# Two feed-forward weight loads moved from behind the fourth key unit to behind the query weights

## The chip, the core and the metric

The kernel runs on one core of one Trainium2 chip, alone. The metric is the device time of one execution in microseconds (us); lower is better. Everything is float32.

## What is computed

One token (x, 512 numbers) goes through two branches, and a sigmoid gate mixes them. Cut from the reference to what matters:

```python
g = sigmoid((x * gate_w).sum())
q = (x @ wq)                                  # 32 query heads of 128; wq is 512 x 4096
scores = q . k_cache / sqrt(128)              # 8 key heads (4 queries share one), 32768 keys each
o = softmax(scores) @ v_cache                 # 8 value heads, 32768 x 128 each
a = o.reshape(4096) @ wo                      # wo is 4096 x 512
h = silu(x @ w1) * (x @ w3)                   # w1, w3 are 512 x 1792
b = h @ w2                                    # w2 is 1792 x 512
out = g * a + (1 - g) * b
```

The caches are by far the largest operands: 8 heads x 32768 x 128 x 4 bytes = 134 MB of keys and as much of values. All weights together are 28 MB. Each byte is read once.

## The kernel before

**Units.** Keys and values come from HBM in units of 8 MiB (128 partitions x 16384 floats), each as one DMA of the SP queue, and into one of two buffers: `big_a` and `big_b`, each of exactly one unit. There are 16 key units, written k0 to k15 here, and 16 value units, v0 to v15. Four key units make up two heads (index `w`, four of them); `t` runs over the key units. wq is as large as a unit and is loaded into `big_a`; w1 and w3 (3.5 MiB each) share `big_b`.

**Order of the loads before.** wq, k0, k1, k2, k3, w1, w3, k4, v0, k5, v1, and so on in turn up to k15 and v11; then v12 to v15, w2 and wo. The function `where(t)` (line 324) names the buffer of a key unit: k0 and k2 go to `big_b`, all others to `big_a`. Values go to `big_b`, the last four alternate. SP issues the loads in this order and waits before each one until the buffer's earlier content has been read.

**Work on one key unit** (`set_aside`, `scores`, lines 336 to 370). A unit has two halves (z = 0, 1) of four chunks. VectorE (DVE) transposes each chunk in 32 x 32 blocks into one of two small buffers (`kt`, one of them inside the tensor `aside`), and TensorE (PE) multiplies it with a window of query columns (`winc`) and sums into a PSUM bank. ScalarE (ACT) copies three of the second half's four chunks into `aside` as soon as the unit has landed, so that the load's buffer is free once DVE has done five of the eight transposes, and PE the five products. SP's next load into that buffer waits for this fifth product. For k3 alone the kernel before also has ACT copy the remaining chunk to an unused corner of `big_b` behind w3 (`extra`, line 340), since k3 and k4 both go to `big_a`.

**After four key units** PE transposes the finished scores (`turn`), and DVE takes the maximum and subtracts it (`softmax`, lines 397 to 421); ACT takes the exponential. The sum over the probabilities (`total`) follows after the next unit. Each engine works through its own list in the order in which the program adds the steps: DVE's part of a softmax stands ahead of its transposes of the next key unit.

**Lag.** `LAG` is 4: values are multiplied four units behind the keys. So PE's work has two loops: one over k0 to k3 without values (with a filler product, line 614, after every second chunk), one over k4 to k15, in which v0 to v11 are multiplied (`values_all`, line 445). A value load waits until PE has multiplied the content of `big_b`.

**The feed-forward branch.** `hidden_products` (line 475) multiplies x with w1 and w3, on PE; `hidden` (line 490) applies silu and the product, on ACT and DVE, and leaves the result for the end. Before, the loads stand behind k3, the products between PE's two loops, and `hidden` behind unit t = 4.

**Recording.** Steps are recorded by `Program.add`, which derives the waits from the names of what a step reads and writes, and are emitted per engine in the order of recording. Line 199 is the helper of nearly all loads of SP, line 432 issues the value units v0 to v11.

Of the kernel before, what the change touches and what calls it, by code (L numbers as in the profile page):

```python
# [118 lines left out]
def kernel(  # L119
# [13 lines left out]
    nc = tc.nc  # L133
    _, HKV, S, DH = k_cache.shape
    D = x.shape[-1]
    F = w1.shape[1]
    HQ = wq.shape[1] // DH
    REP = HQ // HKV
    NC = D // P
# [6 lines left out]
    NB = 64  # L146
    R = NB * DH
    NP = HKV // 2
    NH = 4 * NP
    LAG = 4  # L150
# [7 lines left out]
    pe, dve, act, pool = (  # L158
        lambda fn, _e=e, **kw: pr.add(_e, fn, **kw) for e in ("PE", "DVE", "ACT", "POOL")
    )  # L160
    V, A, T = nc.vector, nc.scalar, nc.tensor

    def sbuf(name, *shape):
        return nc.alloc_sbuf_tensor(name, [P, *shape], F32)[:]

    big = [sbuf("big_a", 2 * R), sbuf("big_b", 2 * R)]
# [28 lines left out]
    def load(dst, src, writes, over=()):  # L195
        lanes[0] += 1
        lane = f"load{lanes[0] % 9}"
        return pr.add(
            "SP", lambda: nc.sync.dma_start(dst, src), writes=writes, over=[*over, lane], inc=lane, by=16, also=lane,  # L199
        )  # L200

    def region(b, z):
        return big[b][:, z * R:(z + 1) * R]
# [7 lines left out]
    ident, ones, fold = sbuf("ident", P), sbuf("ones", P), sbuf("fold", 32)  # L211
# [1 line left out]
    spot, mask, xp = sbuf("spot", 8, 4, 4), sbuf("mask", 32), sbuf("xp", NC, 32)  # L213
    here, share, mine, weight = sbuf("here", 8, 4), sbuf("share", 8, 4), sbuf("mine", 32), sbuf("weight", 2)
    gate, sums, recip, on = sbuf("gate", 2), sbuf("sums", 32), sbuf("recip", 32), sbuf("on", 32)
    mt, mtt, mark, mark2 = sbuf("mt", 32), sbuf("mtt", 128), sbuf("mark", 1), sbuf("mark2", 1)
    high, top = sbuf("high", 1), sbuf("top", 32)
    G = nc.gpsimd
    pool(lambda: G.memset(acc, 0.0), writes=["acc"])  # L219
# [44 lines left out]
    def clear(**kw):  # L264
        pe(zeros,
           reads=["acc"], writes=["s"], **kw)
# [15 lines left out]
    for c in range(NC):  # L282
        def part(c=c):
# [18 lines left out]
         reads=["gate0"], writes=["gate1"])  # L302
# [4 lines left out]
    for b in range(2):  # L307
        qt = kt[b][:, 0:512]
        dve(lambda b=b, qt=qt: V.transpose(qt, rows[b]), reads=[f"row{b}"], writes=[f"kt{b}"])
        for j in range(4):  # L310
            w, u = divmod(4 * b + j, 2)
            src = qt[32 * j:32 * j + 32, :].rearrange("p (q c x) -> p x c q", q=4, c=4)[:, 0]
            for e in range(2):
                r, o = 2 * u + e, 16 + 8 * e + 4 * u
# [7 lines left out]
    vd = v_cache.rearrange("a h (e p n) d -> (a h) e p (n d)", e=2, p=P)  # L322

    def where(t):
        return 1 if t in (0, 2) else 0

    def load_keys(t):
        b = where(t)
        load(big[b], kd[t // 4, t % 4], ["AB"[b] + str(z) for z in range(2)])
# [1 line left out]


    spare = aside.rearrange("p (n r) -> p n r", n=NB)
    extra = big[1][:, 2 * NC * F:2 * R].rearrange("p (n r) -> p n r", n=NB)

    def set_aside(t):
        src, key = region(where(t), 1).rearrange("p (n r) -> p n r", n=NB), "AB"[where(t)] + "1"
        act(lambda: A.copy(spare, src[:, :, 32:128]), reads=[key], writes=["wo"])  # L338
        if t == LAG - 1:
            act(lambda: A.copy(extra, src[:, :, 0:32]), reads=[key], writes=["extra"], over=["B1"])  # L340

    def window(t, z):
        return act(
            lambda: A.copy(winc, win[:, t // 4, :, 16 - 16 * z:48 - 16 * z]),  # L344
            reads=[("win", t // 4, r) for r in range(4)], writes=["winc"], credit="windows",
        )

    def scores_part(c):
        for g in range(4):
            ins = T.matmul(  # L350
                ps_s[32 * g:32 * g + 32, :], winc[:, c, :], kt[c % 2][:, 512 * g:512 * g + 512],
                start=False, stop=False, skip_group_check=True,
            )
        return ins

    def scores(t, z, win_op):
        kin = region(where(t), z).rearrange("p (n c j) -> p c n j", c=4, j=32)
        ks = []
        for c in range(4):
            src, key = kin[:, c], "AB"[where(t)] + str(z)  # L360
            if (z, c) >= (1, 1):
                src, key = spare[:, :, 32 * (c - 1):32 * (c - 1) + 32], "wo"
            elif z == 1 and t == LAG - 1:
                src, key = extra, "extra"
            dst = kt[c % 2].rearrange("p (n i) -> p n i", i=32)
            k = dve(lambda d=dst, s=src: V.transpose(d, s), reads=[key], writes=[f"kt{c % 2}"],  # L366
                    over=["kt0"] * (t >= LAG and (z, c) == (1, 1)), credit="keys")
            pe(lambda c=c: scores_part(c), reads=[f"kt{c % 2}", "winc"], writes=["s"], loop=True,
               credits=((win_op, 1), (k, 1)) if c == 0 else ((k, 1),))
            ks.append(k)  # L370

        if t == LAG - 1 and z == 0:
            done = dve(lambda: V.tensor_copy(mark2, ones[:, 0:1]), reads=["ones"], writes=["mark2"])
            for k in ks:
                k.via = done

    def scores_out(t):
        o = act(
            lambda: A.copy(sb[:, :, :, t % 4], ps_s.rearrange("p (n i) -> p n i", i=32)),  # L379
            reads=["s"], writes=[("sb", t % 4)], credit="scores",  # L380
        )
        return o
# [9 lines left out]
    def turn(loop, credits=()):  # L392
        for f in range(4):
            pe(lambda f=f: turn_part(f), reads=[("sb", m) for m in range(4)] + ["ident"], writes=[f"f{f}"], loop=loop,
               credits=credits if f == 0 else ())
# [33 lines left out]

    def load_values(s):  # L430
        return pr.add(
            "SP", lambda: nc.sync.dma_start(big[1], vd[s // 2, s % 2]), writes=["B0", "B1"], over=["extra"],
            credit="values", by=16,
        )

# [35 lines left out]
    def load_hidden():  # L471
        for z, t in enumerate((w1, w3)):
            load(big[1][:, z * NC * F:(z + 1) * NC * F], t.rearrange("(p c) f -> p (c f)", c=NC), [f"B{z}"])

    def hidden_products():
        for z in range(2):
            def ff(z=z):
                t = big[1][:, z * NC * F:(z + 1) * NC * F]
                for c in range(NC):
                    for j in range(4):  # L480
                        o = c * F + FJ * j
                        ins = T.matmul(
                            pm[z][32 * j:32 * j + 32, 0:FJ], xp[:, c, :], t[:, o:o + FJ],
                            start=(c == 0), stop=(c == NC - 1),
                        )
                return ins
            pe(ff, reads=[f"B{z}", "xp"], writes=[f"m{z}"])


    def hidden():  # L490
        act(lambda: A.activation(silu[:, 0:FJ], pm[0][:, 0:FJ], AF.Sigmoid), reads=["m0"], writes=["tmp0"])
        dve(lambda: V.tensor_mul(silu[:, 0:FJ], silu[:, 0:FJ], pm[0][:, 0:FJ]), reads=["m0", "tmp0"], writes=["tmp0"])
        dve(lambda: V.scalar_tensor_tensor(
            prod[:, 0:FJ].rearrange("p (k a) -> p k a", k=FR), silu[:, 0:FJ].rearrange("p (a k) -> p k a", k=FR),
            gate[:, 1:2], pm[1][:, 0:FJ].rearrange("p (a k) -> p k a", k=FR), op0=ALU.mult, op1=ALU.mult,
        ), reads=["tmp0", "gate1", "m1"], writes=["tmp1"])
        dve(lambda: V.transpose(htp.rearrange("p k a -> p (k a)"), prod[:, 0:FJ]), reads=["tmp1"], writes=["htp"])
# [4 lines left out]
    def store(e, src, key, inc):  # L502
        i, q = (0, nc.scalar) if e == "ACT" else (1, nc.sync)
        pr.add(e, lambda: q.dma_start(outs[2 * i:2 * i + 2, :], src[31 + 64 * i:33 + 64 * i, :]),
               reads=[key], writes=[("out", i)], inc=inc, by=16)

    load_keys(0)
    vals = {}
    first = window(0, 0)
    for t in range(NH):  # L510
        v = t - LAG
        set_aside(t)
        scores(t, 0, first)
        scores(t, 1, window(t, 1))
        out_op = ((scores_out(t), 1),)
        if v < 0:
            clear(loop=True, credits=out_op)
        if t == LAG - 1:
            load_hidden()
        if t + 1 < NH:  # L520
            load_keys(t + 1)
            first = window(t + 1, 0)
        if v >= 1:
            own(v - 1)
        if t % 4 == 3:
            turn(v >= 0, out_op if v >= 0 else ())
        if v >= 0:
            values_loop(vals.pop(v), weights(v), () if t % 4 == 3 else out_op)
            clear(loop=True)
        if t == LAG - 1:  # L530
            hidden_products()
        if v + 1 >= 0 and t + 1 < NH:
            vals[v + 1] = load_values(v + 1)

        if t == NH - 1:
            pool(lambda: G.memset(otp, 0.0), writes=["otp"], over=["kt1"])
        if t % 4 == 3:
            softmax(t // 4)
        if t % 4 == 0 and t > 0:
            total(t // 4 - 1)  # L540
        if t == LAG:
            hidden()
    total(NP - 1)


# [89 lines left out]
    def down(ks):  # L635
# [9 lines left out]
        reads=[("each", 0), ("each", 1), "otp"], writes=["lay"])  # L645
# [38 lines left out]
    done = pr.semaphore("PE")  # L684
# [65 lines left out]
```

## Time and profile before

| | |
|---|---|
| Median of 3 runs | 694.33 us (693.72 to 694.63) |
| Profiled execution: its own time | 694.08 us |
| Span in its trace | 692.4 us |
| Bytes read from HBM | 296.23 MB, 428 GB/s over the span |
| PE / DVE / ACT busy | 402.8 / 368.4 / 134.6 us (58 / 53 / 19 % of the span) |
| SP's load queue | busy for 99.1 % of the span of 16 DMA engines |

In the page's part on queues the last number of a row is the time that the packets of a queue took, as a share of all 16 DMA engines over the span. Times inside a trace are counted from the span's start. A row of a timeline gives start, duration, engine, line, operation, out<-in with shapes, the count of merged instructions, and in brackets how long the engine had been idle and what released it. A load has two rows of interest: its issue on SP, and the first instruction that it released, whose start is called its landing here.

### The profile page before, as it was taken

Reading aid. Unit: us, or ns where it says so; the run is one execution under the profiler, and the core shown is the slowest. Engines: PE = TensorE matmul, PEld = TensorE weight load, DVE = VectorE, ACT = ScalarE, POOL = GpSimd, SP = SyncE. Lnnn points to the kernel's source line nnn. Section 1 sums busy time; section 2 is a strip of 40 time slices with the busy share of each in tenths; the row PEclk is TensorE's granted clock in tenths of the full one; section 3 lists DMA queues with packets and bytes.
Section 4 is the critical chain, followed back from the end, with each engine's and each line's share of the span. In section 5 each row is a group of like instructions: output and inputs, shape, how many; then the busy total and the mean of one; then the engine's idle time right before and its main releaser. Section 6 shows DMA issues by size and latency. Waiting matters only on the chain. (4 is left out here: it accounts for less than half of the span.)

```text
span 692.4 us, 5704 instructions
## 1 busy us (share of the span) xinstructions
PE 402.8 (58%) x2430; PEld 94.6 (14%) x2430; DVE 368.4 (53%) x229; ACT 134.6 (19%) x113; POOL 8.1 (1%) x34
## 2 busy tenths in 40 slices
PE   1537777566474656557484645666573646744575
PEld 0101111201010110201010101201010102211121
DVE  0049999394735637493726537593826546700026
ACT  0143223232303130220303131210303131100000
POOL 4000000000000000000000000000000000000000
PEclk9969999958667676977786777778586777776689
DMA  9999999999999999999999999999999999999996
GB/s 386 455 428 424 424 424 436 448 443 424 428 428 428 435 454 432 424 432 428 432 454 435 424 428 428 432 435 451 432 424 428 428 435 454 435 421 424 433 421 284
DMA packets 6068, 296.34 MB, mean 428 GB/s; under 512 B 678, under 2 KB 682, under 8 KB 1068
## 3 DMA queue, kind: packets, MB, share of 16 engines
q1 hardware_dynamic: 6052, 296.23, 99.1%
q8 instruction: 5, 0.08, 0.0%
q14 instruction: 3, 0.02, 0.0%
q10 hardware_dynamic: 8, 0.01, 0.0%
HBM read 296.23 MB, written 0.00 MB: 428 GB/s over the span
## 5 line engine op out<-in xcount | busy, mean ns | idle before, releaser
L366 DVE STREAM_TRANSPOSE aside<-big_a 128x2048 f32<-128x2048 f32 x41 | 94.3, 2300 | 166.9 <-DMA big_a<-in_A_k_cache_dram 166.9
L350 PE MATMUL ps<-aside,winc 128*32 128x512 f32 x512 | 96.0, 830 | 142.4 <-PEq L688 141.5
L350 PE MATMUL ps<-kt,winc 128*32 128x512 f32 x512 | 96.2, 832 | 61.2 <-PEq L688 61.2
L451 PE MATMUL ps<-big_b,pv 128*32 128x512 f32 x768 | 96.1, 657 | 17.5 <-PEq L688 17.5
L338 ACT COPY aside<-big_a 128x6144 f32<-128x6144 f32 x14 | 74.4, 5313 | 151.8 <-DMA big_a<-in_A_k_cache_dram 151.8
L366 DVE STREAM_TRANSPOSE kt<-aside 128x2048 f32<-128x2048 f32 x32 | 73.4, 2293 | 17.2 <-PE ps L350 17.2
L366 DVE STREAM_TRANSPOSE kt<-big_a 128x2048 f32<-128x2048 f32 x28 | 63.5, 2269 | 0.0
L379 ACT COPY sb<-ps 128x512 f32<-128x512 f32 x16 | 17.1, 1069 | 156.8 <-PE ps L350 156.8
L350 PEld LDWEIGHTS ps<-aside,winc 128*32 128x32 f32 x512 | 13.4, 125 | 215.7 <-issue 215.7
L451 PEld LDWEIGHTS ps<-big_b,pv 128*32 128x32 f32 x768 | 27.7, 120 | 88.1 <-issue 88.1
L366 DVE STREAM_TRANSPOSE aside<-aside 128x2048 f32<-128x2048 f32 x16 | 36.3, 2269 | 0.0
L583 DVE TENSOR_TENSOR sb<-ps,own_b 128x512 f32<-128x512 f32 x2 | 1.4, 691 | 60.8 <-PE ps L574 60.8
L350 PEld LDWEIGHTS ps<-kt,winc 128*32 128x32 f32 x512 | 13.3, 123 | 143.8 <-issue 143.8
L574 PE MATMUL ps<-big_b,probs 128*32 128x512 f32 x128 | 18.0, 726 | 18.8 <-DMA big_b<-in_A_v_cache_dram 18.8
L344 ACT COPY winc<-win 128x128 f32<-128x128 f32 x32 | 9.8, 306 | 78.7 <-PE ps L350 78.7
L574 PE MATMUL ps<-big_a,probs 128*32 128x512 f32 x128 | 17.3, 703 | 10.1 <-DMA big_a<-in_A_v_cache_dram 10.1
L614 PE MATMUL ps<-win,ones 128*128 128x512 f32 x42 | 22.7, 635 | 0.0
L366 DVE STREAM_TRANSPOSE aside<-big_b 128x2048 f32<-128x2048 f32 x7 | 16.0, 2291 | 11.4 <-DMA big_b<-in_A_k_cache_dram 11.4
L262 PE MATMUL ps<-acc 128*128 128x512 f32 x34 | 20.0, 670 | 2.5 <-POOL acc L219 1.6
L400 DVE TENSOR_REDUCE mt<-turned 128x8 f32<-128x2048 f32 x4 | 9.2, 2291 | 22.6 <-PE turned L389 22.6
L424 DVE TENSOR_REDUCE sums<-probs 128x8 f32<-128x2048 f32 x4 | 15.2, 3801 | 2.1 <-ACT probs L417 2.1
L288 PE MATMUL turned<-big_a,xp 128*32 128x512 f32 x64 | 8.5, 691 | 12.1 <-DMA big_a<-in_A_wq_dram 12.1
(93 smaller groups left out, 186.6 us busy)
## 6 DMA issues: line engine op xcount, KB each, us to landing
big_b<-in_B_w_dram SPq DMA_DIRECT2D x2, 3584.0 KB, 20.8
big_a<-in_A_wo_dram SPq DMA_DIRECT2D x1, 4096.0 KB, 27.6
aside<-in_B_w_dram SPq DMA_DIRECT2D x1, 3584.0 KB, 37.4
big_a<-in_A_wo_dram SPq DMA_DIRECT2D x1, 1792.0 KB, 31.5
big_a<-in_A_wo_dram SPq DMA_DIRECT2D x1, 1024.0 KB, 33.5
big_a<-in_A_wo_dram SPq DMA_DIRECT2D x2, 512.0 KB, 34.7
big_a<-in_A_wo_dram SPq DMA_DIRECT2D x1, 256.0 KB, 35.2
big_a<-in_A_k_cache_dram SPq DMA_DIRECT2D x14, 26.3
```

The lines of the kernel that those rows point to most:

```text
L262: return T.matmul(ps_s, acc[:, 0:P], acc, start=True, stop=False, skip_group_check=True)
L288: ins = T.matmul(pf[b][32 * j:32 * j + 32, :], xp[:, c, :], t[:, o:o + REP * DH], start=(c == 0), stop=(c == NC - 1),)
L338: act(lambda: A.copy(spare, src[:, :, 32:128]), reads=[key], writes=["wo"])
L344: lambda: A.copy(winc, win[:, t // 4, :, 16 - 16 * z:48 - 16 * z]),
L350: ins = T.matmul(ps_s[32 * g:32 * g + 32, :], winc[:, c, :], kt[c % 2][:, 512 * g:512 * g + 512], start=False, stop=False, skip_group_chec ...
L366: k = dve(lambda d=dst, s=src: V.transpose(d, s), reads=[key], writes=[f"kt{c % 2}"], over=["kt0"] * (t >= LAG and (z, c) == (1, 1)), cred ...
L379: lambda: A.copy(sb[:, :, :, t % 4], ps_s.rearrange("p (n i) -> p n i", i=32)),
L400: dve(lambda: V.tensor_reduce(mt[:, 0:8], turned.rearrange("p (n q) -> p q n", q=8), axis=AX.X, op=ALU.max), reads=banks, writes=["mt"])
L424: dve(lambda: V.tensor_reduce(sums[:, 8 * w:8 * w + 8].rearrange("p (u q) -> p u q", u=2), probs[:, :, 0:1024].rearrange("p u (n q) -> p u ...
L451: ins = T.matmul(ps_o[32 * t:32 * t + 32, :], pv[:, o:o + 32], big[1][:, n * P:(n + 4) * P], start=((z, g) == (0, 0)), stop=((z, g) == (1, ...
L574: ins = T.matmul(ps_o[32 * t:32 * t + 32, :], prob[u][:, o:o + 32], vt[:, n * P:(n + 4) * P], start=((e, z, g) == (0, 0, 0)), stop=((e, z, ...
L614: return T.matmul(bank[:, 0:n], ones, win.rearrange("p w c n -> p (w c n)")[:, 0:n], start=True, stop=True)
```

## The change

w1 and w3 are issued right behind wq, ahead of k0; both are multiplied on PE behind the query and gate products, ahead of PE's first loop, and `hidden` follows at once. The key units k0 and k2 now go to `big_a`, k1 and k3 to `big_b`. k4 and all later ones stay in `big_a`, values in `big_b`. With that k3 and k4 are in different buffers, and the extra copy of k3's chunk and the small DVE copy that belonged to it (`mark2`) are gone.

```diff
     def where(t):
-        return 1 if t in (0, 2) else 0
+        return 1 if t in (1, 3) else 0
...
     spare = aside.rearrange("p (n r) -> p n r", n=NB)
-    extra = big[1][:, 2 * NC * F:2 * R].rearrange("p (n r) -> p n r", n=NB)
 
     def set_aside(t):
         src, key = region(where(t), 1).rearrange("p (n r) -> p n r", n=NB), "AB"[where(t)] + "1"
         act(lambda: A.copy(spare, src[:, :, 32:128]), reads=[key], writes=["wo"])
-        if t == LAG - 1:
-            act(lambda: A.copy(extra, src[:, :, 0:32]), reads=[key], writes=["extra"], over=["B1"])
...
             if (z, c) >= (1, 1):
                 src, key = spare[:, :, 32 * (c - 1):32 * (c - 1) + 32], "wo"
-            elif z == 1 and t == LAG - 1:
-                src, key = extra, "extra"
...
-        if t == LAG - 1 and z == 0:
-            done = dve(lambda: V.tensor_copy(mark2, ones[:, 0:1]), reads=["ones"], writes=["mark2"])
-            for k in ks:
-                k.via = done
...
+    load_hidden()
     load_keys(0)
+    hidden_products()
+    hidden()
     vals = {}
     first = window(0, 0)
     for t in range(NH):
...
-        if t == LAG - 1:
-            load_hidden()
         if t + 1 < NH:
             load_keys(t + 1)
             first = window(t + 1, 0)
...
-        if t == LAG - 1:
-            hidden_products()
...
-        if t == LAG:
-            hidden()
```

SP's first ten loads (names as above; `B_w1`, `B_w3` are w1 and w3), before:

```order
L199 DMA big_a<-in_A_wq_dram 128x16384
L199 DMA big_b<-in_A_k_cache_dram 128x16384
L199 DMA big_a<-in_A_k_cache_dram 128x16384
L199 DMA big_b<-in_A_k_cache_dram 128x16384
L199 DMA big_a<-in_A_k_cache_dram 128x16384
L199 DMA big_b<-in_B_w1_dram 128x7168
L199 DMA big_b<-in_B_w3_dram 128x7168
L199 DMA big_a<-in_A_k_cache_dram 128x16384
L432 DMA big_b<-in_A_v_cache_dram 128x16384
L199 DMA big_a<-in_A_k_cache_dram 128x16384
```

And with the change, where line 422 is the value load:

```order
L199 DMA big_a<-in_A_wq_dram 128x16384
L199 DMA big_b<-in_B_w1_dram 128x7168
L199 DMA big_b<-in_B_w3_dram 128x7168
L199 DMA big_a<-in_A_k_cache_dram 128x16384
L199 DMA big_b<-in_A_k_cache_dram 128x16384
L199 DMA big_a<-in_A_k_cache_dram 128x16384
L199 DMA big_b<-in_A_k_cache_dram 128x16384
L199 DMA big_a<-in_A_k_cache_dram 128x16384
L422 DMA big_b<-in_A_v_cache_dram 128x16384
L199 DMA big_a<-in_A_k_cache_dram 128x16384
```

w1 and w3 stand second and third, not sixth and seventh; the five key loads keep their order and close ranks, so that nothing stands between k3 and k4.

PE's list around the products of w1 and w3 (`ps<-big_b,xp`). Before, at the end of the first loop (L701), behind the turning of the scores (L389) and ahead of the second loop (L707):

```order
L262 MATMUL ps<-acc 128x512
L701 REGISTER_ALU
L701 COMPARE_AND_BRANCH
L389 MATMUL turned<-ident,sb 128x128 x16
L482 MATMUL ps<-big_b,xp 32x448 x32
L707 ISA
```

With the change, behind the query products (L288) and the gate product (L299), ahead of the first loop (L688):

```order
L288 MATMUL turned<-big_a,xp 32x512 x32
L299 MATMUL ps<-gsm,ones 128x1
L472 MATMUL ps<-big_b,xp 32x448 x32
L688 ISA
L688 UNCONDITIONAL_BRANCH
L678 UNCONDITIONAL_BRANCH
```

DVE's list between the last transpose of k3 and the first of k4, before:

```order
L366 STREAM_TRANSPOSE kt<-aside 128x2048
L400 TENSOR_REDUCE mt<-turned 128x8
L403 STREAM_TRANSPOSE mtt<-mt 32x32 x4
L405 TENSOR_REDUCE high<-mtt 32x1
L408 STREAM_TRANSPOSE top<-high 32x32 x4
L410 TENSOR_TENSOR turned<-turned,top 128x2048
L366 STREAM_TRANSPOSE aside<-big_a 128x2048
```

And with the change (line 361 is the transpose of `scores`):

```order
L361 STREAM_TRANSPOSE kt<-aside 128x2048
L390 TENSOR_REDUCE mt<-turned 128x8
L393 STREAM_TRANSPOSE mtt<-mt 32x32 x4
L395 TENSOR_REDUCE high<-mtt 32x1
L398 STREAM_TRANSPOSE top<-high 32x32 x4
L400 TENSOR_TENSOR turned<-turned,top 128x2048
L361 STREAM_TRANSPOSE aside<-big_a 128x2048
```

Nothing moved here: the first softmax stands between k3 and k4 in both.

More of the change, by code (lines that the diff above doesn't have):

```diff
@@ L215 @@
     gate, sums, recip, on = sbuf("gate", 2), sbuf("sums", 32), sbuf("recip", 32), sbuf("on", 32)
-    mt, mtt, mark, mark2 = sbuf("mt", 32), sbuf("mtt", 128), sbuf("mark", 1), sbuf("mark2", 1)
+    mt, mtt, mark = sbuf("mt", 32), sbuf("mtt", 128), sbuf("mark", 1)
     high, top = sbuf("high", 1), sbuf("top", 32)
@@ L431, in load_values @@
         return pr.add(
-            "SP", lambda: nc.sync.dma_start(big[1], vd[s // 2, s % 2]), writes=["B0", "B1"], over=["extra"],
+            "SP", lambda: nc.sync.dma_start(big[1], vd[s // 2, s % 2]), writes=["B0", "B1"],
             credit="values", by=16,
```

## The prediction

> **What bounds the kernel now.** First the page's queue part (queue: packets, MB, share of 16 engines), then the windows view cut at landings of key units (length, busy time of PE, PEld, DVE, ACT, POOL, then granted clock, DMA share, GB/s):
>
> ```profile
> q1 hardware_dynamic: 6052, 296.23, 99.1%
> 43.71:63.07 19.36, 13.71 (x71) 2.75 (x72) 17.73 (x8) 5.97 (x3) 0.00 (x0) 0.84 1.00 433
> 63.07:82.42 19.35, 13.90 (x76) 2.98 (x74) 17.67 (x9) 6.75 (x5) 0.00 (x0) 1.00 1.00 434
> 101.76:138.14 36.38, 23.42 (x158) 7.07 (x156) 24.20 (x20) 12.56 (x11) 0.00 (x0) 0.96 1.01 434
> 138.14:176.85 38.71, 22.53 (x130) 4.49 (x130) 23.95 (x12) 9.11 (x7) 0.00 (x0) 0.72 1.00 433
> ```
>
> The load queue is never empty. A unit of 8.39 MB lands every 19.35 us whatever the engines do, two take 38.71, and w1 and w3 take 36.38 - 19.35 = 17.03. PE, DVE and ACT each idle somewhere, but only an idle load queue costs time. The next view, PE's timeline, gives the first and the last landing of a load:
>
> ```profile
> 23.21 8.50 PE L288 MATMUL turned<-big_a,xp 128*32 128x512 f32 x64 [12.06 <-DMA big_a<-in_A_wq_dram]
> 688.58 1.05 PE L661 MATMUL turned<-big_a,kt 128*32 128x128 f32 x24 [0.19 <-DMA big_a<-in_A_wo_dram]
> ```
>
> From k0's landing (43.71) to the last one of wo (688.5) 296.23 - 2 x 8.39 = 279.5 MB arrive in 644.8 us, 433 GB/s: the pace of the single windows, so there is no gap in between. What is left are the first 43.7 us and 3.9 us behind the last landing, which the change leaves alone. As the same bytes are loaded after the change, the order by itself can win nothing: the question is whether each load is still issued before the one ahead of it lands.
>
> SP's timeline (issues) shows how much cover there is before:
>
> ```profile
> 0.99 0.40 SPq L199 DMA_DIRECT2D big_a<-in_A_wq_dram  x1
> 1.44 0.41 SPq L199 DMA_DIRECT2D big_b<-in_A_k_cache_dram  x1
> 31.77 0.33 SPq L199 DMA_DIRECT2D big_a<-in_A_k_cache_dram  x1
> 56.13 0.33 SPq L199 DMA_DIRECT2D big_b<-in_A_k_cache_dram  x1
> 92.57 2.52 SPq L199 DMA_DIRECT2D big_b<-in_B_w_dram  x2
> 110.72 0.33 SPq L199 DMA_DIRECT2D big_a<-in_A_k_cache_dram  x1
> 131.02 0.33 SPq L432 DMA_DIRECT2D big_b<-in_A_v_cache_dram  x1
> 150.94 0.33 SPq L199 DMA_DIRECT2D big_a<-in_A_k_cache_dram  x1
> 168.65 0.33 SPq L432 DMA_DIRECT2D big_b<-in_A_v_cache_dram  x1
> ```
>
> These are wq, k0, k1, k2, (w1, w3), k4, v0, k5, v1. DVE's timeline gives the landings of k0, k1, k3, k4 and k5 (bracket with a DMA) and what DVE does from k3 to k5:
>
> ```profile
> 43.71 2.31 DVE L366 STREAM_TRANSPOSE aside<-big_b 128x2048 f32<-128x2048 f32 x1 [9.67 <-DMA big_b<-in_A_k_cache_dram]
> 63.07 2.31 DVE L366 STREAM_TRANSPOSE aside<-big_a 128x2048 f32<-128x2048 f32 x1 [1.63 <-DMA big_a<-in_A_k_cache_dram]
> 101.76 2.31 DVE L366 STREAM_TRANSPOSE aside<-big_a 128x2048 f32<-128x2048 f32 x1 [1.69 <-DMA big_a<-in_A_k_cache_dram]
> 117.22 2.27 DVE L366 STREAM_TRANSPOSE kt<-aside 128x2048 f32<-128x2048 f32 x1
> 124.85 2.29 DVE L400 TENSOR_REDUCE mt<-turned 128x8 f32<-128x2048 f32 x1 [5.37 <-PE turned L389]
> 129.35 2.30 DVE L410 TENSOR_TENSOR turned<-turned,top 128x2048 f32<-128x2048 f32 x1
> 138.14 2.31 DVE L366 STREAM_TRANSPOSE aside<-big_a 128x2048 f32<-128x2048 f32 x1 [6.49 <-DMA big_a<-in_A_k_cache_dram]
> 157.63 3.78 DVE L424 TENSOR_REDUCE sums<-probs 128x8 f32<-128x2048 f32 x1
> 176.85 2.31 DVE L366 STREAM_TRANSPOSE aside<-big_a 128x2048 f32<-128x2048 f32 x1 [11.30 <-DMA big_a<-in_A_k_cache_dram]
> ```
>
> k2 is issued 56.13 - 43.71 = 12.42 us after k0 landed, 63.07 - 56.13 = 6.9 us before k1 lands; later issues have as much. What I read here above all is the 6.49 us of idle time ahead of k4: DVE ends the first softmax at 131.65, 29.89 us after k3 landed, and k4 lands 36.38 us after k3. The 17.03 us of w1 and w3 between the two units cover the softmax.
>
> **The change part by part.** *The start.* wq, w1 and w3 are issued together at 1 to 2 us. By bytes w3 lands 0.875 of a unit after wq: at 23.2 + 17.0 = 40.2 by the steady pace, at 23.2 + 0.875 x 20.5 = 41.1 by the pace of the second load before (43.71 - 23.21 = 20.5). k0 needs `big_a`, read by the query products; the row at 31.77 is this very wait, so k0 is issued 8 us before the queue runs dry. Its cost is nothing; were those 8 us gone, each further us would count in full. k1 needs `big_b`, so both products:
>
> ```profile
> 124.74 6.22 PE L482 MATMUL ps<-big_b,xp 128*32 128x448 f32 x64
> ```
>
> Half of that, 3.1 us, comes after w3's landing: k1 is issued at about 44.3, 15 us before k0 lands (40.2 + 19.35 = 59.6). silu's three DVE steps and one ACT step fall into DVE's 9.67 us and more of idle time before k0. Cost nothing.
>
> *k0 to k3.* k0 lands some 16 us later than before and every unit 19.35 us after the last, as before; issue comes 12.4 after a landing, 6.9 before the next one. Alternating the buffers keeps this cover. Cost nothing.
>
> *k3 to v0.* Let K be k3's landing. SP, waiting for k3's fifth product, issues v0 at K + 12.4; k4 lands at K + 19.35, v0 at K + 38.71. Two instructions vanish (busy time, mean ns | idle time before them, in the groups by line):
>
> ```profile
> L340 ACT COPY big_b<-big_a 128x2048 f32<-128x2048 f32 x1 | 1.9, 1908 | 0.0
> L373 DVE COPY mark<-ones 128x1 f32<-128x1 f32 x1 | 0.1, 109 | 0.0
> ```
>
> 1.9 us on ACT beside DVE's transposes of k3's first half (9 us), so not on the path, and 0.1 us on DVE, which puts the softmax's end 0.1 us earlier at most; I leave it out.
>
> *k4 and k5.* This is where the cover goes. k4 now lands at K + 19.35, but in DVE's list it still stands behind the softmax, which ends at K + 29.89: its eight transposes, the 5.4 us until PE has turned the scores, and 6.8 us of softmax are all set by k3. So DVE starts k4 at K + 29.9, 10.5 us late. ACT is not later:
>
> ```profile
> 133.03 1.94 ACT L417 ACTIVATE probs<-turned 128x1024 f32<-128x1024 f32 x2
> 138.14 5.31 ACT L338 COPY aside<-big_a 128x6144 f32<-128x6144 f32 x1 [3.18 <-DMA big_a<-in_A_k_cache_dram]
> ```
>
> the exponential ends at K + 33.2 and the copy of k4 at K + 38.5, ahead of DVE's fifth transpose. From DVE's start to the issue of the next key load it took 150.94 - 138.14 = 12.80 us here; 12.41 at other units:
>
> ```profile
> 215.54 2.31 DVE L366 STREAM_TRANSPOSE aside<-big_a 128x2048 f32<-128x2048 f32 x1 [18.93 <-DMA big_a<-in_A_k_cache_dram]
> 227.96 0.33 SPq L199 DMA_DIRECT2D big_a<-in_A_k_cache_dram  x1
> ```
>
> I take 12.80, since PE stands as idle ahead of k4 as before (9 us). k5 is issued at K + 29.89 + 12.80 = K + 42.7, while v0, the last load in the queue, lands at K + 38.7: 4.0 us too late. Behind k5 SP has v1, which also waits; so the queue is empty.
>
> To this comes the time in which a load that starts in an empty queue moves nothing. The trace of before has only one such load, wq: 23.21 - 0.99 = 22.22 us from issue to landing. Against 19.35 that is 2.87 us; against the 20.5 us of the second load, if the slow part of the start is a slow pace, 1.7. A small transfer bounds it too, the store of the result on SP:
>
> ```profile
> 690.02 0.33 SPq L504 DMA_DIRECT2D out_dram<-winc  x1
> ```
>
> it is issued at 690.02 and the span ends at 692.4, so all of it is under 2.4 us. I take the middle of 1.7 and 2.87, 2.3.
>
> The stall is 4.0 + 2.3 = 6.3 us; bounds (4.0 - 0.4) + 1.7 = 5.3, with 12.41 for 12.80, and 4.0 + 2.87 = 6.9.
>
> The Trainium skill, page "DMA: Bandwidth & Descriptors", section "Anatomy of one DMA — SWDGE (gpsimd) path", fits a DMA as about 2.0 us plus its bytes at 436 GB/s, most of the 2.0 being completion (fitted for loads that GpSimd issues; these are SP's). For a unit that is an estimate of 21.2 us, 1.9 above 19.35, and the stall would be 5.9; the wq row, with 22.22, is above it.
>
> *Behind the stall.* k5 lands at K + 38.71 + 19.35 + 6.3 = K + 64.4. v1 waits for PE's products with v0: 168.65 - 138.14 = 30.5 us after DVE starts k4, so K + 60.4, 4.0 before k5 lands, enough. DVE ends k4 and `total` at K + 29.9 + (161.4 - 138.1) = K + 53.2, so k5 is read at once. From there the spacing of a key unit is 38.7 us again, the next softmax lies in the 39 us between two key units, and all waits are as before: the end shifts by the stall, with nothing that gives it back.
>
> **Sum.** Profiled execution 694.08 us (span 692.4, the rest lies around it), 0.25 below the median of 694.33, well within the spread of the three runs. 694.08 + 6.3 = 700.4 us.
>
> **Rivals.**
>
> *The stall is given back* (not slower). Place: the load queue from k5 on. If 433 GB/s is what SP asks for and not what the engines can move, later units land faster than 19.35 apart until the 6.3 us are made up: 694.1 us. It decides only if the queue can go over 433 once it is behind. For it speaks the page's row of 40 slices:
>
> ```profile
> GB/s 386 455 428 424 424 424 436 448 443 424 428 428 428 435 454 432 424 432 428 432 454 435 424 428 428 432 435 451 432 424 428 428 435 454 435 421 424 433 421 284
> ```
>
> Some slices are at 454. Against it: they stand between slices at 424, and whole units land 19.35 apart although the next load was queued 7 us before. The Trainium skill, page "DMA: Bandwidth & Descriptors", section "Where 436 GB/s comes from", gives 435 GB/s as the ceiling of the ports into SBUF, which the trace's 433 bears out; it also says that the HBM side, at about 358, binds such loads, which the trace contradicts. Chance of this rival: 6 %.
>
> *The start gets shorter.* k0 took 20.5 us instead of 19.35. If this belongs to a key unit that is queued behind wq, and not to the start, up to 1.2 us come back; with the stall 699.2, within my range, without any stall 692.9. I give the second 3 %.
>
> *PE is slow when it turns k3's scores.* At the second softmax, with a lower clock, DVE's maximum starts later after its key unit:
>
> ```profile
> 254.25 2.31 DVE L366 STREAM_TRANSPOSE aside<-big_a 128x2048 f32<-128x2048 f32 x1 [17.00 <-DMA big_a<-in_A_k_cache_dram]
> 279.19 2.29 DVE L400 TENSOR_REDUCE mt<-turned 128x8 f32<-128x2048 f32 x1 [4.83 <-PE turned L389]
> ```
>
> 24.94 us against 124.85 - 101.76 = 23.09. That adds 1.9: 702.3. Against it: the first loop, with its fillers, ran at a granted clock of 1.00 (the 63.07 window), and it is unchanged. 8 %.
>
> **How the numbers follow.** Forecast (stall at k5, not given back) 83 %, slow turning 8, given back 6, shorter start without stall 3. Predicted 700.4. Low: 694.08 + 5.3 - 1.2 = 698.2; high: the slow turning, 702.3; a little on each side for the runs' spread, 698.0 to 702.5. About 0.2 % (1.4 us) is what a measurement of this kernel can tell from no change: slower 0.91, same 0.06, faster 0.03.
>
> **What would show it.** In the changed profile: k0 issued near 31.8 and landing near 60; landings 19.35 apart up to v0; DVE's softmax directly followed by k4's first transpose with no DMA wait in between; SP's issue of k5 about 4 us after v0's landing, and k5 landing some 25.6 us after it instead of 19.35; DMA below 433 GB/s in that one window; all else shifted by the same amount. I am wrong if k5 is issued before v0 has landed, if the units behind it land less than 19.35 us apart, or if a gap shows up at the start.

## The result and the profile after

The changed kernel takes 701.04 us (median of 4 runs, 700.68 to 701.36), the kernel before on the same chip 694.06 us: a ratio of 1.0102 (95 % interval 1.009 to 1.0115), slower by 7.0 us. The profiled execution took 701.03 us with a span of 699.3, against 694.08 and 692.4.

The page's queue row and its row of 40 slices (17.5 us each), after:

```profile
q1 hardware_dynamic: 6052, 296.23, 98.2%
GB/s 409 403 443 427 431 457 424 428 361 345 435 420 420 427 469 424 420 420 465 435 420 420 446 454 420 420 431 469 420 420 420 450 450 420 420 440 454 421 410 289
```

The same packets and bytes, and the queue's share falls from 99.1 to 98.2 %: it stood empty. The hole lies in the ninth and tenth slice, 140 to 175 us, at 361 and 345 GB/s. The windows view after, cut at the landings of k3, of v0 (2 x 19.35 us after k3's), of k5 and of k6 (columns: window and length; busy us and instructions of PE, PE's weight loads, DVE, ACT and POOL; granted clock, DMA share, GB/s):

```profile
118.46:157.17 38.71, 21.95 (x118) 5.74 (x116) 32.98 (x23) 15.97 (x11) 0.00 (x0) 0.87 0.94 407
157.17:182.67 25.50, 16.80 (x106) 3.72 (x106) 12.69 (x6) 1.97 (x4) 0.00 (x0) 0.80 0.89 370
182.67:221.53 38.86, 21.27 (x130) 4.34 (x130) 18.49 (x10) 7.29 (x6) 0.00 (x0) 0.79 1.00 432
```

One unit takes 25.50 us from v0's landing instead of 19.35, which is 6.15 us. SP's timeline after, from k4 to v2:

```profile
111.45 0.33 SPq L199 DMA_DIRECT2D big_a<-in_A_k_cache_dram  x1
130.81 0.33 SPq L422 DMA_DIRECT2D big_b<-in_A_v_cache_dram  x1
160.73 0.33 SPq L199 DMA_DIRECT2D big_a<-in_A_k_cache_dram  x1
180.19 0.33 SPq L422 DMA_DIRECT2D big_b<-in_A_v_cache_dram  x1
195.08 0.33 SPq L199 DMA_DIRECT2D big_a<-in_A_k_cache_dram  x1
214.43 0.33 SPq L422 DMA_DIRECT2D big_b<-in_A_v_cache_dram  x1
```

k5 is issued at 160.73; v0 landed at 157.17. DVE's timeline after shows what k5 waited for:

```profile
118.46 2.31 DVE L361 STREAM_TRANSPOSE aside<-big_b 128x2048 f32<-128x2048 f32 x1 [1.69 <-DMA big_b<-in_A_k_cache_dram]
133.85 2.27 DVE L361 STREAM_TRANSPOSE kt<-aside 128x2048 f32<-128x2048 f32 x1
141.49 2.29 DVE L390 TENSOR_REDUCE mt<-turned 128x8 f32<-128x2048 f32 x1 [5.37 <-PE turned L379]
145.99 2.30 DVE L400 TENSOR_TENSOR turned<-turned,top 128x2048 f32<-128x2048 f32 x1
148.32 2.31 DVE L361 STREAM_TRANSPOSE aside<-big_a 128x2048 f32<-128x2048 f32 x1
182.67 2.31 DVE L361 STREAM_TRANSPOSE aside<-big_a 128x2048 f32<-128x2048 f32 x1 [11.54 <-DMA big_a<-in_A_k_cache_dram]
```

The row at 148.32 is k4's first transpose. It has no bracket: DVE went from the softmax straight to k4, which had landed at 118.46 + 19.35 = 137.81. Before, the same row had 6.49 us of idle time ahead of it.

With K for k3's landing, the steps against the prediction:

| | predicted | measured |
|---|---|---|
| k0 issued, landed | 31.8, 59.6 | 32.68, 60.41 |
| DVE starts k4 | K + 29.9 | K + 29.86 |
| k5 issued | K + 42.7 | K + 42.27 |
| behind v0's landing | 4.0 | 3.56 |
| k5 landed | K + 64.4 | K + 64.21 |
| stall | 6.3 | 6.15 |
| v1 issued | K + 60.4 | K + 61.73 |
| time | 700.4 | 701.04 |

### The profile page after: what moved, and what is told of

Its sections match the earlier page's. It is cut to its first block, busy times and chain, and to the rows that moved or that the text cites. A ratio compares the mean times of both kernels' runs of the same rounds, so it can differ in the third digit from the quotient of the medians.

```text
span 699.3 us, 5701 instructions
## 1 busy us (share of the span) xinstructions
PE 397.4 (57%) x2430; PEld 94.8 (14%) x2430; DVE 368.5 (53%) x228; ACT 130.2 (19%) x110; POOL 8.1 (1%) x34
## 3 DMA queue, kind: packets, MB, share of 16 engines
q1 hardware_dynamic: 6052, 296.23, 98.2%
## 5 line engine op out<-in xcount | busy, mean ns | idle before, releaser
L361 DVE STREAM_TRANSPOSE aside<-big_a 128x2048 f32<-128x2048 f32 x42 | 96.6, 2300 | 173.9 <-DMA big_a<-in_A_k_cache_dram 173.2
L347 PE MATMUL ps<-aside,winc 128*32 128x512 f32 x512 | 93.3, 807 | 146.9 <-PEq L675 146.2
L347 PE MATMUL ps<-kt,winc 128*32 128x512 f32 x512 | 93.1, 806 | 62.8 <-PEq L675 62.8
L441 PE MATMUL ps<-big_b,pv 128*32 128x512 f32 x768 | 94.4, 648 | 17.6 <-PEq L675 17.6
L288 PE MATMUL turned<-big_a,xp 128*32 128x512 f32 x64 | 9.4, 752 | 12.0 <-DMA big_a<-in_A_wq_dram 12.0
L361 DVE STREAM_TRANSPOSE aside<-big_b 128x2048 f32<-128x2048 f32 x6 | 13.7, 2283 | 2.5 <-DMA big_b<-in_A_k_cache_dram 2.5
## 6 DMA issues: line engine op xcount, KB each, us to landing
big_b<-in_B_w_dram SPq DMA_DIRECT2D x2, 3584.0 KB, 34.6
```

The source lines that it names most:

```text
L288: ins = T.matmul(pf[b][32 * j:32 * j + 32, :], xp[:, c, :], t[:, o:o + REP * DH], start=(c == 0), stop=(c == NC - 1),)
L347: ins = T.matmul(ps_s[32 * g:32 * g + 32, :], winc[:, c, :], kt[c % 2][:, 512 * g:512 * g + 512], start=False, stop=False, skip_group_chec ...
L441: ins = T.matmul(ps_o[32 * t:32 * t + 32, :], pv[:, o:o + 32], big[1][:, n * P:(n + 4) * P], start=((z, g) == (0, 0)), stop=((z, g) == (1, ...
```

## Experiments

All runs are timed beside the kernel before on their chip; ratios have 95 % intervals. What had to be told apart: whether the softmax between k3 and k4 is the cause (by way of k5's late issue), or the new order of loads and buffers itself; later, how early a load must be issued.

### The first softmax behind k4's fifth transpose

```diff
             ks.append(k)
+            if (t, z, c) == (LAG, 1, 0):
+                softmax(0)
...
-        if t % 4 == 3:
+        if t % 4 == 3 and t != LAG - 1:
             softmax(t // 4)
```

> Edit: the changed kernel, with the first softmax (its VectorE and ScalarE steps) recorded behind the fifth transpose of k4 and not ahead of the first. Theory (the softmax holds k4 back, so k5 is issued into an empty queue): k5 is issued about 12.4 us after k4 lands, 7 us before v0 lands, and the stall of 6.15 us is gone: 694.0 to 694.3 us, or 1 us more if the late loss of 1.1 us between k15 and v13 belongs to the program and not to the stall. v1 is then issued only 2.4 us before k5 lands, which may cost up to 0.3 us. Rival (the loss lies in the new order of loads and buffers itself): 701.0 as before.

Measured: 696.13 us against 694.06, ratio 1.0023 (1.0001 to 1.0045). Some 5 of the 7 us are gone, and with them the stall at k5. SP's and DVE's timelines of this run:

```profile
151.43 0.33 SPq L199 DMA_DIRECT2D big_a<-in_A_k_cache_dram  x1
175.75 0.33 SPq L424 DMA_DIRECT2D big_b<-in_A_v_cache_dram  x1
```

```profile
138.06 2.31 DVE L361 STREAM_TRANSPOSE aside<-big_a 128x2048 f32<-128x2048 f32 x1 [1.68 <-DMA big_a<-in_A_k_cache_dram]
176.75 2.31 DVE L361 STREAM_TRANSPOSE aside<-big_a 128x2048 f32<-128x2048 f32 x1 [10.12 <-DMA big_a<-in_A_k_cache_dram]
217.13 2.31 DVE L361 STREAM_TRANSPOSE aside<-big_a 128x2048 f32<-128x2048 f32 x1 [20.34 <-DMA big_a<-in_A_k_cache_dram]
```

k5 lands 38.69 us after k4: no gap. But the softmax now delays the end of k4, so v1 is issued only 1.0 us ahead of k5's landing, and k6 lands 40.38 us after k5 instead of 38.70. The rival is out; 694.0 to 694.3 was missed. Of what is left in the profiled execution (697.2 us), 1.7 us lie at v1, which the softmax now made late; 0.7 us are lost again between k15's landing and v13's (last section), and 0.4 us at a load further on, for which this run shows no cause.

### One maximum more, half a softmax less

```diff
-        dve(lambda: V.tensor_reduce(mt[:, 0:8], ...)
+        for _ in range(2 if w == 0 else 1):
+            dve(lambda: V.tensor_reduce(mt[:, 0:8], ...)
```

> Edit: the changed kernel with the first softmax's maximum taken twice, 2.3 us more of VectorE ahead of k4. Theory: k5 is issued 2.3 us later into the same empty queue, every us counts: 703.4 us. Rival (the order of loads and buffers): VectorE has room in this stage, 701.0 us.

Measured: 703.81 us, ratio 1.0144 (1.0127 to 1.0161), 2.8 us above the changed kernel where 2.3 were added. In its trace k3 landed at 118.39; SP's and DVE's timelines have k5's issue and landing:

```profile
162.99 0.33 SPq L199 DMA_DIRECT2D big_a<-in_A_k_cache_dram  x1
```

```profile
184.95 2.31 DVE L361 STREAM_TRANSPOSE aside<-big_a 128x2048 f32<-128x2048 f32 x1 [11.59 <-DMA big_a<-in_A_k_cache_dram]
```

k5 was issued at K + 44.6 (2.3 later) and landed 66.56 us after k3 instead of 64.21, 2.35 more. Up to k5's landing, one us more of DVE between k3 and k4 is one us more of time; the 0.4 us beyond that lie elsewhere.

The other way, `softmax` is cut at the subtraction, and only subtraction and exponential go behind the fifth transpose:

```diff
             ks.append(k)
+            if (t, z, c) == (LAG, 1, 0):
+                finish(0)
...
+        if t == LAG - 1:
+            shift(0)
-        if t % 4 == 3:
+        elif t % 4 == 3:
             softmax(t // 4)
```

> Edit: the changed kernel with only the first softmax's subtraction (2.3 us on VectorE) and the exponential behind k4's fifth transpose. Theory: k5 is issued 1.3 us after v0 landed and not 3.6, with the same 2.6 us for the start in an empty queue: a stall of 3.8 us, 698.7 us. Rival: 701.0 us.

Measured: 700.01 us (698.95 to 701.69), ratio 1.0091 (1.0073 to 1.0109); expected were 698.7. SP's and DVE's timelines of this run, in which k3 landed at 118.74:

```profile
158.74 0.33 SPq L199 DMA_DIRECT2D big_a<-in_A_k_cache_dram  x1
```

```profile
180.89 2.31 DVE L361 STREAM_TRANSPOSE aside<-big_a 128x2048 f32<-128x2048 f32 x1 [10.84 <-DMA big_a<-in_A_k_cache_dram]
```

k5 is issued 1.3 us after v0's landing and lands 62.15 us after k3, a stall of 62.15 - 58.05 = 4.1 us, close to the theory's 3.8. The rest came one unit later: k6 landed 40.69 us after k5, 2.0 too many, although v1 had been issued 2.9 us ahead of k5's landing. So the stall behaves as reckoned, and the need of 2.6 us ahead is not the whole truth.

### The same stall in the kernel before

```diff
-        dve(lambda: V.tensor_reduce(mt[:, 0:8], ...)
+        for _ in range(8 if w == 0 else 1):
+            dve(lambda: V.tensor_reduce(mt[:, 0:8], ...)
```

> Edit: the kernel before the change, with the first softmax's maximum taken eight times, 16.2 us more of VectorE, which is nearly what w1 and w3 take between k3 and k4. Theory: the softmax ends 46.1 us after k3 landed, k5 is issued at 58.5 to 58.9, v0 lands at 55.7, so with 2.6 us for the empty queue a stall of 5.4 to 5.8 us: 699.5 to 700 us, in the old order of loads. Rival (only the new order of loads loses): 694.1 us.

Measured: 701.1 us, ratio 1.0102 (1.0085 to 1.0119). DVE's and SP's timelines of this run, the old order of loads with a long softmax:

```profile
145.48 2.30 DVE L411 TENSOR_TENSOR turned<-turned,top 128x2048 f32<-128x2048 f32 x1
147.81 2.31 DVE L366 STREAM_TRANSPOSE aside<-big_a 128x2048 f32<-128x2048 f32 x1
182.65 2.31 DVE L366 STREAM_TRANSPOSE aside<-big_a 128x2048 f32<-128x2048 f32 x1 [7.39 <-DMA big_a<-in_A_k_cache_dram]
```

```profile
160.61 0.33 SPq L199 DMA_DIRECT2D big_a<-in_A_k_cache_dram  x1
```

The picture is that of the changed kernel to within 0.6 us, without its order of loads: DVE starts k4 at 147.8, k5 is issued at 160.6 and lands at 182.7. v0 landed at 101.62 + 36.38 + 19.35 = 157.35, so k5 came 3.3 us late and landed 5.95 us late. 16.2 us of added DVE work do what taking away 17.0 us of transfer did.

### Spreading the softmax, and fillers

The next runs ask how early a load has to be issued. First, the softmax in three steps behind k4's fourth, fifth and sixth transpose (`most`: the maximum; `spread`: the small steps; `finish`: subtraction and exponential):

```diff
             ks.append(k)
+            step = {(0, 3): most, (1, 0): spread, (1, 1): finish}.get((z, c))
+            if t == LAG and step:
+                step(0)
```

> Edit: the changed kernel, with the first softmax cut in three and spread over k4: the maximum behind the fourth transpose, the small steps behind the fifth, subtraction and exponential behind the sixth. Theory (each load must be issued some 2.7 us before the one ahead of it lands): k5 is issued 14.7 us after k4 landed, 4.6 us ahead of v0; v1 comes with PE cold some 36 to 37 us after k4, 2 us ahead of k5's landing, which costs 0 to 1.5 us: 694.0 to 695.6 us. Rival (what was left in the late-softmax run is a cost of loads beside the softmax, not of v1's lead): 696.1 us as there.

Measured: 696.29 us, ratio 1.0036 (1.0022 to 1.005). k5 was issued at 153.51, 3.6 us ahead of v0's landing (19.35 us after k4's) and not 4.6, and landed 2.1 us late all the same, 0.3 of which were v0's; v1, 3.6 us ahead of k5, cost 0.2.

The same with PE's fillers in the second loop:

```diff
-                if warm and c % 2:
-                    spend(ps_o, 512)
+                if c % 2:
+                    spend(bank, 512)        # ps_o in the first loop, pm[0] in the second
```

> Edit: the same, and PE's second loop with the filler product of the first loop behind every second chunk, into a bank that is free there. Theory: PE stays at full clock, the products with v0 take 7.1 us and not 8.7, v1 is issued 3 us or more ahead of k5's landing, and no load is late: 694.0 us, as before the change. Rival (loads beside the softmax cost by themselves): 696.1 us.

Measured: 695.4 us, ratio 1.0018 (1.0008 to 1.0028). The products with v0 took 7.07 us as expected, yet v1 came 3.75 us ahead of k5's landing and cost 1.0 us, and k5, 4.5 us ahead of v0's, cost 0.8. Neither 694.0 nor 696.1.

The fillers alone, on the changed kernel:

> Edit: the changed kernel with the fillers in PE's second loop alone. Theory: the softmax still holds k4, k5 is still issued 3.6 us after v0 landed; only v1's lead grows to some 4 us: 700.8 to 701.0 us. Rival (PE's clock is behind the loss): 695 to 697 us.

Measured: 701.5 us, ratio 1.011 (1.0093 to 1.0127); expected 700.8 to 701.0. PE's timeline of this run and the matching row of the changed kernel:

```profile
170.96 7.07 PE L441 MATMUL ps<-big_b,pv 128*32 128x512 f32 x64 [0.92 <-PEq L675]
```

```profile
171.44 8.69 PE L441 MATMUL ps<-big_b,pv 128*32 128x512 f32 x64 [1.93 <-PEq L675]
```

The granted clock over these products was 1.00, in the changed kernel 0.81. v1 was issued 4.7 us ahead of k5's landing instead of 2.5, and nothing was won. PE's clock is not behind the loss.

### How much cover is enough

Four more maxima in the kernel before (the edit above with 5 for 8):

> Edit: the kernel before the change, with the first softmax's maximum taken five times, 9.3 us more of VectorE. Theory: the softmax ends 39.2 us after k3 landed, so DVE starts k4 2.8 us late, but k5 is issued at 51.6 to 52.0 while v0 lands at 55.7, a lead of 3.7 to 4.1 us, which is enough: 694.1 us. Rival (every us that k4 waits for the softmax counts): 696.9 us; (every load that is issued less than 7 us ahead costs): 695 or more.

Measured: 695.77 us, ratio 1.002 (1.001 to 1.003): both loads that were expected to be early enough cost something, k5 0.6 us with 3.7 us ahead, v1 0.5 us with 4.1; another 0.9 us is lost at k13, which was issued 6.75 us ahead (an instruction block passes there, see the last section). So with three more (4 for 8), k4 still a little late:

> Edit: the kernel before the change, with the first softmax's maximum taken four times, 7.0 us more of VectorE. What the runs so far suggest: issues that came 4.5 us or less ahead of the landing before them cost 0.1 to 2 us each, those 4.7 us and more ahead cost nothing. Here DVE starts k4 0.5 us late, k5 is issued some 6 us ahead of v0's landing and v1 6 us or more ahead of k5's: 694.1 us. Rival (a fixed need of 2.7 us, and what the run with four more lost came from elsewhere, in proportion to the delay): 695.3 us.

Measured: 693.88 us against 693.94, ratio 0.9995 (0.9987 to 1.0004). SP's and DVE's timelines of this run:

```profile
151.13 0.33 SPq L199 DMA_DIRECT2D big_a<-in_A_k_cache_dram  x1
169.53 0.33 SPq L433 DMA_DIRECT2D big_b<-in_A_v_cache_dram  x1
```

```profile
138.72 2.31 DVE L366 STREAM_TRANSPOSE aside<-big_a 128x2048 f32<-128x2048 f32 x1
177.02 2.31 DVE L366 STREAM_TRANSPOSE aside<-big_a 128x2048 f32<-128x2048 f32 x1 [11.95 <-DMA big_a<-in_A_k_cache_dram]
215.73 2.31 DVE L366 STREAM_TRANSPOSE aside<-big_a 128x2048 f32<-128x2048 f32 x1 [18.66 <-DMA big_a<-in_A_k_cache_dram]
```

7 us more of DVE work cost nothing, and k4 waited for DVE (no bracket at 138.72), if only for 0.4 us. Delay at k4 costs only by way of the loads behind it, k5 6.4 and v1 7.5 us ahead here; with four more, k4 was read 2.8 us late and the two loads behind it lost 1.1 us.

All leads of this stretch, from the traces (lead: issue ahead of the landing of the load in front, v0's taken as 19.35 us after k4's; cost: what the next key unit landed later than 19.35 us per unit, so that a row of v1 takes in the key unit k6):

| run | load | lead, us | cost, us |
|---|---|---|---|
| changed, one more maximum | k5 | -5.9 | 8.5 |
| changed | k5 | -3.6 | 6.2 |
| changed with fillers | k5 | -3.6 | 6.1 |
| before, seven more | k5 | -3.3 | 6.0 |
| changed, half | k5 | -1.3 | 4.1 |
| late softmax | v1 | 1.0 | 1.7 |
| changed; before, seven more; changed, one more | v1 | 2.5, 2.6, 2.7 | 0.2, 0.3, 0.0 |
| changed, half | v1 | 2.9 | 2.0 |
| spread | k5; v1 | 3.6; 3.6 | 2.1; 0.2 |
| before, four more | k5; v1 | 3.7; 4.1 | 0.6; 0.5 |
| spread with fillers | v1; k5 | 3.75; 4.5 | 1.0; 0.8 |
| changed with fillers | v1 | 4.7 | 0.2 |
| no first maximum (below) | k5; v1 | 4.7; 6.4 | 0.0; 0.0 |
| before, three more | k5; v1 | 6.4; 7.5 | 0.1; 0.0 |

From the latest issue to a lead of 1.0 us, cost and lead add up to 2.5 to 2.8 us: that is the price of an empty queue, the prediction's 2.3. Between 2.5 and 4.5 us the cost is irregular, 0 to 2 us; from 4.7 us on it is at most 0.2.

The landings of all units (last section) bear out the 4.7: in the twelve traces 44 unit loads behind the first ones were issued 4.67 to 6.5 us ahead, and none of them landed more than 0.03 us late. They also show where a long lead does not help: of the loads issued earlier still, some landed 0.2 to 1.1 us late, mostly where an instruction block passed; eight of them, all in runs in which k5 or v1 had been late, lost 0.2 to 0.5 us without one, and why stays open. The 0.2 of v1 with fillers is of this kind: it fell on k6, issued 6.9 us ahead.

### The order of loads by itself

```diff
+        if w > 0:
             dve(lambda: V.tensor_reduce(mt[:, 0:8], ...)
...                                            # and the other DVE steps of softmax, indented
```

> Edit: the changed kernel without the VectorE part of the first softmax: the exponential of the first two heads is taken of the raw scores, so their maximum is neither found nor subtracted (left out work: 6.8 us of VectorE, once). Theory (the new order of loads and buffers costs nothing, only the softmax between k3 and k4 does): DVE goes straight from k3 to k4, k5 is issued 7 us ahead of v0, v1 8 us ahead of k5, every load lands 19.35 us after the last: 693.7 to 694.1 us. Rival (weights first, or k3 and k4 in different buffers, costs by itself): 695 us or more.

Measured: 694.22 us against 693.94, ratio 1.0003 (0.9994 to 1.0011). DVE's timeline of this run:

```profile
118.58 2.31 DVE L361 STREAM_TRANSPOSE aside<-big_b 128x2048 f32<-128x2048 f32 x1 [1.69 <-DMA big_b<-in_A_k_cache_dram]
137.93 2.31 DVE L361 STREAM_TRANSPOSE aside<-big_a 128x2048 f32<-128x2048 f32 x1 [1.69 <-DMA big_a<-in_A_k_cache_dram]
176.63 2.31 DVE L361 STREAM_TRANSPOSE aside<-big_a 128x2048 f32<-128x2048 f32 x1 [13.59 <-DMA big_a<-in_A_k_cache_dram]
215.34 2.31 DVE L361 STREAM_TRANSPOSE aside<-big_a 128x2048 f32<-128x2048 f32 x1 [18.95 <-DMA big_a<-in_A_k_cache_dram]
```

k4 is read as it lands, and the units from k3 to k6 land 19.35 us apart. Weights first, buffers alternating and no softmax on DVE in between: the time of the kernel before, with nothing won and nothing lost. (k5's issue came 4.7 us ahead and not 7: DVE's sixth transpose waited 3.24 us for PE here. It was enough.)

No version beat the kernel before. Between the landing of k0 and the last one of wo it has no gap for another order of loads to close.

## Why the prediction was right

**Direction and mechanism.** The bound was read rightly as the load queue, and the cover rightly as the 6.49 us ahead of k4: the change takes 17 us of transfer out of the place where the first softmax needs them. The runs with one maximum more and with half a softmax move the stall by what was added or taken, the kernel before shows the same stall with a softmax made longer, and without the softmax's DVE part the change costs nothing.

**The start costs nothing:** right, and even 0.3 us were won: k3's landing plus a unit is 137.81 after, where the kernel before has, by bytes, 138.14. The times within it were off: the query products took 9.40 us, not 8.50, and the second half of the w1 and w3 products 4.91, not 3.1, so k0 was issued at 32.68 and k1 at 46.04. Both waits had room.

**The stall at k5:** the term was 4.0 + 2.3 = 6.3 us, and measured 3.56 + 2.59 = 6.15. I had taken 12.80 us from DVE's start to the next key load, arguing that PE would be as cold as before; it took 12.41, the other end. The empty queue was 2.5 to 2.8 us in the five runs with a real stall, nearer the upper end, 2.87, that the wq row had given. One part of the term was 0.44 too long and the other 0.29 too short, so their sum came out better than either; that is luck.

**v1 "4.0 us before k5 lands, enough":** it was 2.5, since the products with v0 took 8.69 us at a granted clock of 0.81 and not the 7.08 of before, at 1.00; PE began them 23.1 us after DVE's start of k4, where it had been 23.4. It cost 0.2 us. That this passes for enough was luck: other runs paid up to 2 us for leads of that size.

**"The end shifts by the stall, with nothing that gives it back":** here a step failed, on the other side. From k5's landing on 0.2 us (v1) and another 1.1 us were lost. The windows view after, from k15's landing in steps of two units and one, and below it v13's window before:

```profile
570.14:608.85 38.71, 25.03 (x149) 6.37 (x150) 29.37 (x24) 9.13 (x7) 0.95 (x1) 0.76 1.00 433
608.85:629.29 20.44, 9.30 (x66) 2.19 (x66) 3.55 (x5) 0.00 (x0) 0.00 (x0) 0.75 0.98 421
```

```profile
602.98:622.35 19.37, 9.54 (x67) 2.44 (x66) 4.15 (x7) 0.00 (x0) 0.00 (x0) 0.76 1.00 431
```

v13 took 20.44 us instead of 19.37, although it had been issued at 602.09, 6.8 us ahead. The sum of the shifts is -0.3 + 6.15 + 0.2 + 1.1, about 7.1; the last landing of wo moved from 688.58 to 695.53, by 6.95, the difference being an earlier, smaller hiccup that both kernels have (k13 to k14: 39.10 us before, 39.01 after). So the forecast of 700.4 is 0.6 below the 701.04 measured because the prediction has no term for the 1.1 us, which the shorter start and the slightly shorter stall made up in part. What is behind the 1.1 us is the subject of the last section.

**The rivals.** The stall was not given back: from k6 to k13 units land 19.35 us apart after it as before. PE was not slow in turning k3's scores: DVE waited 5.37 us for them, as before. No time came back at the start beyond 0.3 us: by the completions (last section) k0 took 1.3 us more than 19.35 before, with an instruction block of 16 KB passing at 34.6, and w3 took 1.0 us more than its bytes need after, with one at 36.9.

## What to carry to other kernels

When a queue of transfers is the bound, moving a transfer wins nothing, but the transfer is also a pause for the engines between the loads around it: before moving it, see which engine's work lies in its shadow and which load waits for that engine. What counts is the lead of each issue over the landing in front of it, and not by itself how late a unit is read: here a unit read 0.4 us late cost nothing with the loads behind it issued 6.4 us ahead and more. In these runs a lead of 4.7 us was enough, about the price of an empty queue (2.6) and the spread of the transfer engines (2) together; that it is this sum that counts is not shown.

## What the runs showed of the hardware

**A landing is that of the slowest of 16 DMA engines.** Each load ends with 16 completions, one per engine; the trace keeps their times, without the engine's name. For three loads around the stall and two late ones, first and last of the 16 completions in us from the span's start (worked out from the trace's records; DVE's first row of before's k4, at 138.14, follows the last completion by 0.02):

```
                        first     last    spread
before  k4             136.04   138.12     2.07
before  v0             155.45   157.47     2.02
before  k5             174.81   176.83     2.02
before  v12            600.50   602.96     2.46
before  v13            619.85   622.31     2.46
after   v0             155.56   157.19     1.63
after   k5             181.85   182.65     0.80
after   v12            607.92   608.82     0.90
after   v13            627.27   629.25     1.98
```

Before, the engines stay 2.0 to 2.5 us apart from k0's landing on, and the first completion as well as the last come 19.35 us after those of the unit ahead. So the slowest engine sets all landings. When the queue runs dry, all engines start the next load almost together (the first packets of k5 in the changed kernel between 161.70 and 162.45), and the spread falls to 0.8.

At v13 one engine of the changed kernel falls behind by 1.5 us: of the 16 completions, counted from the first, the one at 0.44 is gone and one at 1.98 has come. The spread grows from 0.90 to 1.98, and the landing comes 1.1 us later. In the kernel before an engine falls behind by as much in the same unit (0.50 is gone, 2.01 has come), but the slowest one is at 2.46, and the landing does not move. At that place both traces show the transfer of a block of 16 KB of a kind that the profile calls "instruction", at 612.73 in the changed kernel and at 607.72 in the kernel before, 1.07 and 1.02 us long. As each ends, a data packet of 64 KB starts (613.79 and 608.72) and takes 2.92 and 2.97 us, where 2.42 is the median. Block and slow packet together make up the 1.5 us. The profile's page counts these blocks in its row on instruction transfers, here after:

```profile
q8 instruction: 6, 0.10, 0.1%
```

The other traces fit. Where the spread at v12's landing was 1.67 us or less (the changed kernel 0.90, late softmax 1.07, one more maximum 1.20, before with seven more 1.55, changed with fillers 1.67), 0.65 to 1.1 us are lost from v13 to v15; in the seven traces where it was 2.1 us or more, nothing is. One of the seven is half the softmax, which had a stall at k5 but a spread of 2.66 later: that speaks for the small spread as the cause, and not for the stall itself. The smaller loss that both kernels have at k13 to k14 lies at a block of 8 KB (497.50 and 503.37). All this is read from the traces; no run took an instruction block away.

**An early issue can still cost.** With engines 2 us apart, the first ones run out of work 2 us before the landing, so that 2.6 + 2 us of lead would be needed to keep all of them busy, which is near the 4.7 us from which nothing is lost. A pause of the first engines alone would not move the last one; the packets show that more is at work. In the run with the spread softmax the first 16 packets of k5, issued 3.6 us ahead, start between 155.36 and 157.10, as the 16 engines end v0 (155.15 to 157.00), so there is hardly a pause; but they take 2.46 to 4.35 us instead of 2.42, the latest of them 4.24, and the unit lands late. With half a softmax, v1, issued 2.9 us ahead, is late on a single engine, the last to end k5: it stands still from 180.42 to 181.54, and its first packet takes 3.43 us; together these are 2.1 us, and the cost was 2.0. In the run with three more maxima, with leads of 6.4 and 7.5 us, no packet at the start of k5 or v1 took over 2.5 us. Why packets of a load issued a few us ahead run slowly, and why on the last engine in some runs only, stays open.

**The empty queue.** From issue to landing k5 took 21.89 to 22.15 us in the five runs that stalled there, 2.5 to 2.8 above the 19.35 that it takes in a full queue. The Trainium skill, page "DMA: Bandwidth & Descriptors", section "Anatomy of one DMA — SWDGE (gpsimd) path", has a fixed cost of about 2.0 us, fitted for loads that GpSimd issues; SP's 2.5 to 2.8 are longer here. In the changed kernel k5's first packets start 1.0 to 1.7 us after its issue and take 2.66 to 3.25 us instead of 2.42.
